# Joining two low-rank products and pairing the attention scores under a TensorE-bound MLP

## The chip, the cores and the metric

The kernel runs on one core of a Trainium2 chip. The metric is device time in microseconds (us) of one execution; "before" and "after" are compared by runs that shared a chip. In the profile PE is TensorE's matmuls, PEld its weight loads, DVE VectorE, ACT ScalarE, POOL GpSimd, and SPq/ACTq the queues that issue transfers. L545 is line 545 of the kernel before; the changed kernel keeps these numbers in all lines used here, and some experiments are six or fewer lines longer.

## The reference

Retention over four batches, then a mixer with a low-rank product over the sequence and an MLP.

```python
# q, k, v: (4, 8, 768, 64); gamma per head
state = gamma * state + k_t v_t^T;  y_t = q_t state / sqrt(64)
x = y as (4, 768, 512)
h = x^T @ U @ V            # U: 768x32, V: 32x768
u = x + h^T
out = u + relu(u @ w_ch1) @ w_ch2      # 512 -> 2048 -> 512
```

## The kernel before

The retention is computed in chunks of 128 positions. Batch b's attention is woven into batch b-1's MLP: `weave` lays the MLP's matmul pieces in order and drops other steps (turns, states, scores, mixes) between them where a share of the MLP's work is done. A step's number, such as 0.743, is such a share; steps fall in front of the first piece that begins at or after it. PSUM banks are dealt from rings, and two of the rings that matter hold a single bank.

```python
RINGS = {"mlp": [0, 1, 2], "s": [3, 4], "o": [5], "qk": [6], "st": [7], ...}

def turn_pe(nm, b, sc, xs_=(0, 1)):       # transposes q or k of two chunks
    tp = bank("qk", bf16)
    ...                                   # 4 or 8 transposes into tp (L465)
    if nm == "q": q_order(b, sc, tp)      # ScalarE (batch 1) reads the bank
    else:         evac("A", turned(...), tp[...])

def score_one(b, ci):
    score(b, ci)                          # 8 matmuls of 64 rows into s, s (L506)
    screen(b, ci)                         # VectorE: 2 masked products, a (L516)

def score_two(b, ci):
    score(b, ci + 1, ("mlp", "o"))
    score(b, ci)
    screen(b, ci + 1)
    screen(b, ci)
    ...

def mix(b, ci):
    o_p = bank("o")
    ...                                   # state part L540 (not for ci = 0), a part L545
    evac("A", xs[b][:, ci], o_p)
# ... cut ...
    grow_turned(0)                        # L861, 4 matmuls of 32 rows, then the eviction uT
    keep_busy(3)                          # 12 filler matmuls, L193
    first = [part(lr_expand, 0, 4, 2), part(lr_turn_pe, 0, 4),
             part(lr_expand, 0, 0, 4)]    # L576 matmuls and x additions, woven in
```

GpSimd prepares batch 1's k, q and v (products and casts from transfers that have landed), in a fixed order, behind its casts of the weights.

Of the kernel before, what the change touches and what calls it, by code (L numbers as in the profile page):

```python
# [18 lines left out]
def kernel(  # L19
# [52 lines left out]
    def bank(tag, dtype=fp32):  # L72
        n_bank[0] += 1
        ring = RINGS[tag]
        ring.append(ring.pop(0))
        return psum.tile([P, 2048 // (4 if dtype == fp32 else 2)], dtype,
                         tag=f"bank{ring[-1]}", name=f"{tag}_{n_bank[0]}",
                         bufs=1)
# [103 lines left out]
    idle_bank = [None]  # L182
# [385 lines left out]

    grown = {}

    def lr_grow(b, j0, nj, last="qk"):
        banks = [bank(t) for t in ("s", "s", "o", last)]
        grown[b] = banks
        for j in range(j0, j0 + nj):
            for c in range(NCB):
                nc.tensor.matmul(banks[c][:, ts(j - j0, P)],  # L576
                                 V4[ds(RK * c, RK), ts(j, P)],
                                 pcs[b][ds(RK * c, RK)], start=True, stop=True)
# [277 lines left out]
            nc.tensor.matmul(xT[c][:, ts(j, P)], xs[b][:, j, ts(c, P)], ident16,  # L856
                             start=(j == 0), stop=False, skip_group_check=True)

    def grow_turned(b):
        for c in range(NCB):  # L860
            nc.tensor.matmul(xT[c][:, :LO], pcs[b][ds(RK * c, RK)],  # L861
                             V4[ds(RK * c, RK), :LO], start=False, stop=True,
                             skip_group_check=True)
        for c in range(NCB):
            evac("AD"[c % 2], uTs[b][:, :NLO, c], four(xT[c]))

# [56 lines left out]
    for c in range(1, NCB):  # L923
        x_turn(c, 0)
        x_turn(c, 2)
    idle_bank[0] = bank("s")
    grow_turned(0)
    keep_busy(3)
    first = [part(lr_expand, 0, 4, 2), part(lr_turn_pe, 0, 4),
             part(lr_expand, 0, 0, 4)]  # L930

    prep_keys(1, pair(1, 0)[:AHEAD])
    for j in range(4):
# [1 line left out]
    for b in range(1, B + 1):  # L935
        tracks = []
        if b > 1:
            old = b - 1 < SEVEN
            first = [part(lr_expand, b - 1, 4, 2, "qk" if old else "st"),
                     part(lr_turn_pe, b - 1, 4, "qk" if old else "o")  # L940
                     if b < 3 else part(lr_turn, b - 1, 4)]
            if not old:
                RINGS["mlp"] = [6, 0, 1, 2]
        tracks.append((first, *((0.02, 0.2), (0.02, 0.14), (0.0, 0.06),
                                (0.0, 0.03))[b - 1]))
        if b < B:
            if b == 1:
                at = [0.503, 0.61, 0.675, 0.735, 0.793, 0.845]
                lag = [0.01, 0.035, 0.065]
                for sc in range(NSC):  # L950
                    keys = pair(b, sc)
                    c0, c1 = 2 * sc, 2 * sc + 1
                    if sc:
                        tracks.append(([part(prep_keys, b, keys[:AHEAD])],
                                       at[c0] - 0.1, 1))
                    tracks.append(([part(prep_keys, b, keys[AHEAD:])],
                                   at[c1] - 0.1, 1))
                    for f, d in ((part(turn_pe, "q", b, sc),
                                  at[c0] + (0.035, -0.042, -0.042)[sc]),
                                 (part(turn_pe, "k", b, sc, (0,)),  # L960
                                  at[c0]),
                                 (part(turn_pe, "k", b, sc, (1,)), at[c1])):
                        tracks.append(([f], d, d))
                for sc in range(NSC):
                    tracks.append(([part(prep_keys, 2, pair(2, sc))],
                                   0.752 + 0.03 * sc, 1))
                for i in range(2 * NSC):
                    tracks.append(([part(turn_dma, "kq"[i % 2], 2, i // 2)],
                                   0.84, 0.84))
                for f, d in zip(w2_sums(0) + w2_sums(2) + w2_sums(4),  # L970
                                (0.51, 0.525, 0.54, 0.585, 0.655, 0.67, 0.72,
                                 0.735, 0.78, 0.8, 0.875, 0.895)):
                    tracks.append(([f], d, d))
            else:
                at = [(0.205, 0.06)[b - 2] + (0.074, 0.1)[b - 2] * i
                      for i in range(NCK)]
                lag = [0.0, 0.04, 0.1]
                two = [(0.25, 0.395, 0.595), (0.1, 0.27, 0.44)][b - 2]
                if b == 2:
                    for _ in range(RING):  # L980
                        feed_one(False)
                    steps = [(0.01 + 0.022 * i, f)
                             for i, f in enumerate(w2_sums(6))]
                    steps.append((0.125, part(lr_grow, 1, 0, 4, "st")))
                    steps += [(0.125 + 0.022 * i, part(lr_add, 1, 0, 4, (c,)))
                              for i, c in enumerate((3, 2, 0, 1))]
                    for sc in range(NSC):
                        steps.append((0.57 + 0.08 * sc,
                                      part(prep_keys, 3, pair(3, sc))))
                        for nm in "kq":  # L990
                            if not sc:
                                steps.append((0.64, part(turn_dma, nm, 3, sc)))
                else:
                    steps = [(0.08, part(turn_dma, nm, 3, sc))
                             for sc in (1, 2) for nm in "kq"]
                for d, f in steps:
                    tracks.append(([f], d, d))
            if b > 1:
                for sc in range(NSC):
                    d = two[sc] - (0.04, 0.05, 0.08 if b == 2 else 0.05)[sc]  # L1000
                    tracks.append(([lambda b=b, sc=sc: q_order(
                        b, sc, live["q", b, sc])], d, d))
            for i in range(NCK):
                more = (0.027, 0.0, 0.0, 0.0, 0.0, -0.015)[i]
                late_by = (0.032, 0.0, 0.012, 0.0, 0.01, 0.0)[i]
                if b == 2 and i > 3:
                    p = two[2] + 0.05 * (i - 4)
                    steps = [(state, p - 0.035), (score_one, p),
                             (mix, p + (0.07, 0.047)[i - 4])]
                elif b > 1:  # L1010
                    p = two[i // 2]
                    steps = [(state, p + (-0.035, 0.02)[i % 2]),
                             (mix, p + (0.08, 0.12)[i % 2])]
                    if i % 2 == 0:
                        steps.append((score_two, p))
                else:
                    steps = [(state, at[i] + lag[0]),
                             (score_one, at[i] + lag[1] + more),
                             (mix, at[i] + lag[2] + late_by)]
                for f, d in steps:  # L1020
                    tracks.append(([part(f, b, i)], d, d))
            t = at[-1] + lag[2] if b == 1 else two[-1] + (0.102, 0.122)[b - 2]
            if b == 1:
                turns = [part(x_turn, c, j0, b, tag)
                         for c, tag in enumerate(("qk", "st", "s", "s"))
                         for j0 in (0, 2)]
                for fs, d in ((turns[:4], t + 0.006),
                              ([part(lr_open, b), part(lr_proj, b)], t + 0.022),
                              (turns[4:], t + 0.023),
                              ([part(grow_turned, b)], t + 0.044)):  # L1030
                    tracks.append((fs, d, d))
            else:
                for fs, d in (([part(lr_open, b), part(lr_proj, b)],
                                0.025),
                              ([part(lr_grow, b, 0, 4, "st")], 0.047),
                              ([part(lr_add, b, 0, 4, (0,))], 0.047),
                              ([part(lr_add, b, 0, 4, (1,))], 0.052),
                              ([part(lr_add, b, 0, 4, (2,))], 0.066),
                              ([part(lr_add, b, 0, 4, (3,))], 0.076),
                              ([part(lr_turn, b, 0)], 0.08),  # L1040
                              ([part(lr_turn, b, 2)], 0.081)):
                    tracks.append((fs, t + d, t + d))
        weave(b == 1, mlp_pieces(b - 1), *tracks)
# [29 lines left out]
```

## Time and profile before

| what | before |
|---|---|
| time, median of the first runs | 220.2 us (220.09 to 221.0) |
| span of the profiled execution | 218.6 us |
| TensorE busy | 211.7 us, 97% |
| VectorE, ScalarE, GpSimd busy | 66%, 42%, 38% |
| waits of TensorE, 24 to 84 us | one: first mix on VectorE |

Ends of matmuls are modelled in this profile, so I read TensorE from start to start: what an instruction costs is the distance to the next one's start. A stall is what that distance has over the plain one. A bracket such as `[0.31 <-DVE a L516]` is idle time after the modelled end, so it understates a stall.

### The profile page before, as it was taken

What the parts mean: (1) busy time and instruction counts of PE and PEld (TensorE: products, weight loads), DVE (VectorE), ACT (ScalarE), POOL (GpSimd) and SP (SyncE); (2) the same over time, 40 slices, a digit from 0 to 9 for tenths busy, and PEclk for the clock granted to TensorE, in tenths of its full rate; (3) what the DMA queues carried; (4) which work ended last, traced back from release to release, by engine and by line L of the source; (5) the groups of instructions that cost most, each with busy time, mean ns of one, the idle gap of its engine ahead of it and who ended that gap; (6) DMA issues with size and microseconds to landing.
All of it is one profiled execution on the core that took longest, in us unless ns stands there. A gap on an engine that the chain in (4) does not pass through costs nothing.

```text
span 218.6 us, 5522 instructions
## 1 busy us (share of the span) xinstructions
PE 211.7 (97%) x2239; PEld 147.3 (67%) x2239; DVE 144.3 (66%) x303; ACT 92.8 (42%) x192; POOL 82.3 (38%) x121
## 2 busy tenths in 40 slices
PE   7879999999999999999999999999999999999994
PEld 2568854486556554666788875756888856668884
DVE  6478665334478858699695856598985542867443
ACT  3347745466356424676912005867510035551000
POOL 5457888888686977000069920000000000000000
PEclk9999999999999999999999999999999999999999
DMA  5999999999999999999999789700007240000043
GB/s 166 301 293 294 319 352 276 352 356 244 219 226 220 253 230 213 161 339 250 228 236 164 175 197 182 122 1 3 0 3 181 110 135 9 3 1 0 18 153 120
DMA packets 84489, 38.82 MB, mean 178 GB/s; under 512 B 58384, under 2 KB 77552, under 8 KB 84464
## 3 DMA queue, kind: packets, MB, share of 16 engines
q1 hardware_dynamic: 83456, 36.84, 71.5%
q10 hardware_dynamic: 1008, 1.64, 2.6%
q8 instruction: 17, 0.28, 0.6%
q14 instruction: 8, 0.07, 0.1%
HBM read 27.46 MB, written 6.29 MB: 154 GB/s over the span
## 4 chain that ended last, share of the span: by engine, by line
PE 91%; ACT 3%; DMA 2%; DVE 2%; SPq 1%; issue 0%; ACTq 0%
PE mlp L763 38%; PE A L655 15%; PE mlp L814 9%; PE C L655 6%; PE B L655 4%; DMA in<-in_q_dram 2%; PE o L545 2%; PE s L506 2%; ACT qT L85 2%; PE o L540 1%; PE st L490 1%; PE mlp L193 1%; PE qk L465 1%; PE s L576 1%; PE mlp L363 1%; PE s L404 1%
## 5 line engine op out<-in xcount | busy, mean ns | idle before, releaser
L763 PE MATMUL mlp<-uT,w1b 128*128 128x512 f16 (+1 forms) x512 | 88.6, 326 | 0.0
L773 ACT ACTIVATE gT<-mlp 128x512 f16<-128x512 f32 (+1 forms) x98 | 47.4, 490 | 63.9 <-PE mlp L763 61.7
L763 PEld LDWEIGHTS <-w1b 128*128 128x128 f16 x512 | 48.2, 98 | 30.0 <-POOL w1b L340 0.2
L771 DVE TENSOR_SCALAR gT<-mlp 128x512 f16<-128x512 f32 (+1 forms) x30 | 16.7, 556 | 25.3 <-PE mlp L763 24.7
L655 PEld LDWEIGHTS <-gT 128*128 128x128 f16 x288 | 27.7, 98 | 3.3
L814 PE MATMUL mlp<-w2b,gT 128*128 128x512 f16 x96 | 23.7, 380 | 0.0
L306 POOL TENSOR_TENSOR kd<-in,gk 128x512 bf16<-128x512 f32 x18 | 19.0, 1071 | 5.5 <-DMA in<-in_k_dram 5.5
L516 DVE TENSOR_TENSOR a<-s,mask 128x512 bf16<-128x512 f32 x26 | 16.7, 683 | 6.6 <-PE s L506 6.6
L655 PEld LDWEIGHTS <-gS 128*128 128x128 f16 x200 | 19.2, 98 | 2.6
L306 POOL TENSOR_TENSOR qd<-in,gq 128x512 bf16<-128x512 f32 x18 | 18.9, 1070 | 1.0 <-DMA in<-in_q_dram 1.0
L655 PE MATMUL A<-w2t,gT 128*128 128x256 f16 x144 | 18.4, 273 | 0.0
L85 ACT ACTIVATE state<-st 64x256 bf16<-64x256 f32 x40 | 15.0, 374 | 6.2 <-PE st L386 3.2
L85 ACT ACTIVATE x<-o 128x512 f16<-128x512 f32 x20 | 11.9, 596 | 13.3 <-PE o L545 12.9
L814 PEld LDWEIGHTS <-gT 128*128 128x128 f16 x96 | 8.4, 98 | 7.9 <-issue 0.2
L304 POOL CAST vd<-in 128x512 bf16<-128x512 f32 x18 | 11.4, 649 | 1.3 <-DMA in<-in_v_dram 1.2
L346 POOL CAST w2b<-in 128x512 f16<-128x512 f32 x16 | 9.7, 613 | 1.5 <-DMA in<-in_moe_w_ch_dram 0.6
L608 POOL COPY gate<-gT 128x1 f16<-128x1 f16 x1 | 0.2, 190 | 25.5 <-DVE gT L608 25.5
L340 POOL CAST w1b<-in 128x512 f16<-128x512 f32 x16 | 9.3, 613 | 0.8 <-DMA in<-in_moe_w_ch_dram 0.4
L655 PE MATMUL B<-w2b,gT 128*128 128x256 f16 x72 | 9.3, 273 | 0.0
L655 PE MATMUL A<-w2t,gS 128*128 128x256 f16 x72 | 9.0, 273 | 0.0
L582 DVE TENSOR_TENSOR x<-s,x 128x256 f16<-128x256 f32 (+1 forms) x16 | 8.1, 550 | 1.3 <-issue 0.7
L655 PE MATMUL A<-w2b,gT 128*128 128x256 f16 x72 | 8.8, 273 | 0.0
(156 smaller groups left out, 293.3 us busy)
## 6 DMA issues: line engine op xcount, KB each, us to landing
in<-in_moe_w_ch_dram SPq DMA_DIRECT2D x32, 256.0 KB, 5.2
in<-in_k_dram SPq DMA_DIRECT2D x24, 256.0 KB, 5.4
in<-in_q_dram SPq DMA_DIRECT2D x24, 256.0 KB, 5.0
in<-in_v_dram SPq DMA_DIRECT2D x24, 256.0 KB, 5.4
out_dram<-o SPq DMA_DIRECT2D x16, 256.0 KB, 2.0
out_dram<-o ACTq DMA_DIRECT2D x6, 256.0 KB, 3.1
out_dram<-o SPq DMA_DIRECT2D x3, 128.0 KB, 1.7
Uf<-in_moe_U_dram SPq DMA_DIRECT2D x1, 96.0 KB, 5.4
```

Source lines behind the costliest of these rows:

```text
L85: nc.scalar.activation(dst, src, AF.Copy)
L304: nc.gpsimd.tensor_copy(out=t, in_=src)
L306: nc.gpsimd.tensor_tensor(t, src, g, op=ALU.mult)
L340: nc.gpsimd.tensor_copy(out=w1b[:, c, ts(mb, 512)], in_=take("w1", mb, c))
L346: nc.gpsimd.tensor_copy(out=w2b[:, m], in_=take("w2", m))
L516: nc.vector.tensor_tensor(a, four(sp[i]), causal(mask), op=ALU.mult)
L582: nc.vector.tensor_tensor(us[b][:, ds(j0, nj), ts(c, P)], four(grown[b][c])[:, :nj], xs[b][:, ds(j0, nj), ts(c, P)], op=ALU.add)
L655: nc.tensor.matmul(acc[key, i], lhs[:, m, ts(i, P)], rhs[:, m], start=(fresh and m == 0), stop=(m == NH - 1), skip_group_check=True)
L763: nc.tensor.matmul(g_p[:, :sz], w1b[:, c, ts(m, P)], uTs[b][:, ds(j, nj), c], start=(c == 0), stop=(c == NCB - 1))
L771: nc.vector.tensor_relu(gT[:, m, ds(lo, sz)], g_p[:, :sz])
L773: nc.scalar.activation(gT[:, m, ds(lo, sz)], g_p[:, :sz], AF.Relu)
L814: nc.tensor.matmul(ch, gT[:, m, ts(j, P)], w2b[:, m], start=(m == 0), stop=(m == NM - 1))
```

## The change

It is meant to take array switches (from matmuls on 128 rows to ones on 64 or 32, or back; in the trace of before 0.09 us each: eight L814 and the entry of a score take 1.82 from 53.06 to 54.88, where eight alone take 1.73) and fillers out of TensorE's sequence: batch 0's product for its last two chunks goes beside the turned product in place of the fillers, and batch 1's chunks 0 to 3 are scored in pairs. Mixes, the w2 sums (VectorE's sums of blocks of w2, with which later batches multiply) and one turn of q are moved to fit.

```diff
-    def lr_grow(b, j0, nj, last="qk"):
-        banks = [bank(t) for t in ("s", "s", "o", last)]
+    def lr_grow(b, j0, nj, last="qk", third="o"):
+        banks = [bank(t) for t in ("s", "s", third, last)]
...
-    def grow_turned(b):
+    def grow_turned(b, more=None):
...                                          # the four L861
+        if more:
+            more()
...
-    idle_bank[0] = bank("s")
-    grow_turned(0)
-    keep_busy(3)
-    first = [part(lr_expand, 0, 4, 2), part(lr_turn_pe, 0, 4),
-             part(lr_expand, 0, 0, 4)]
+    grow_turned(0, part(lr_grow, 0, 4, 2, "qk", "st"))
+    lr_add(0, 4, 2)
+    first = [part(lr_turn_pe, 0, 4), part(lr_expand, 0, 0, 4)]
...
-        tracks.append((first, *((0.02, 0.2), ...
+        tracks.append((first, *((0.06, 0.22), ...
...
                     for f, d in ((part(turn_pe, "q", b, sc),
-                                  at[c0] + (0.035, -0.042, -0.042)[sc]),
+                                  at[c0] + (0.035, -0.042, -0.05)[sc]),
...
                 for f, d in zip(w2_sums(0) + w2_sums(2) + w2_sums(4),
-                                (0.51, 0.525, 0.54, 0.585, 0.655, 0.67, 0.72,
-                                 0.735, 0.78, 0.8, 0.875, 0.895)):
+                                (0.51, 0.525, 0.54, 0.555, 0.57, 0.585, 0.6,
+                                 0.615, 0.715, 0.73, 0.745, 0.76)):
...
                     steps = [(state, at[i] + lag[0]),
-                             (score_one, at[i] + lag[1] + more),
-                             (mix, at[i] + lag[2] + late_by)]
+                             (mix, (0.702, 0.724, 0.825, 0.85, 0.88, 0.912)[i])]
+                    if i in (0, 2):
+                        steps.append((score_two, (0.652, 0, 0.775)[i]))
+                    elif i > 3:
+                        steps.append((score_one, (0.842, 0.868)[i - 4]))
```

More of the change, by code (lines that the diff above doesn't have):

```diff
@@ L943 @@
                 RINGS["mlp"] = [6, 0, 1, 2]
-        tracks.append((first, *((0.02, 0.2), (0.02, 0.14), (0.0, 0.06),
+        tracks.append((first, *((0.06, 0.22), (0.02, 0.14), (0.0, 0.06),
                                 (0.0, 0.03))[b - 1]))
@@ L1003 @@
             for i in range(NCK):
-                more = (0.027, 0.0, 0.0, 0.0, 0.0, -0.015)[i]
-                late_by = (0.032, 0.0, 0.012, 0.0, 0.01, 0.0)[i]
                 if b == 2 and i > 3:
```

## The prediction

> **What bounds the kernel now.** I read the page first (busy shares, slices, chain), then the waits of TensorE, then the timelines of the two places that the change edits: the start of batch 0's up-projection (27 to 31 us) and its down-projection, under which batch 1's attention runs (50 to 78 us).
>
> ```profile
> PE 211.7 (97%) x2239; PEld 147.3 (67%) x2239; DVE 144.3 (66%) x303; ACT 92.8 (42%) x192; POOL 82.3 (38%) x121
> ...
> PEclk9999999999999999999999999999999999999999
> ...
> PE 91%; ACT 3%; DMA 2%; DVE 2%; SPq 1%; issue 0%; ACTq 0%
> ```
>
> TensorE is busy 97% of the span at the full granted clock, and 91% of the chain is TensorE. No transfer, and no other engine for long, is between two of its instructions after the first 28 us. The waits of TensorE between 24 and 84 us are one line:
>
> ```profile
> PE o L545 <- DVE a L516: 0.3, 1, 0.3
> ```
>
> So time is saved only by taking instructions, array switches or that one wait out of TensorE's own sequence, and it is lost wherever a new wait is put in.
>
> The timeline at the start of the up-projection (start, length, engine, line, what):
>
> ```profile
> 27.60 0.84 PE L193 MATMUL s<-ones 128*128 128x128 bf16 x12
> 27.70 1.08 ACT L85 ACTIVATE uT<-mlp 128x512 f16<-128x512 f32 x2 [0.94 <-PE o L861]
> ...
> 28.34 0.68 DVE L87 CAST uT<-o 128x512 f16<-128x512 f32 x1
> 28.34 1.11 PE L763 MATMUL mlp<-uT,w1b 128*128 128x512 f16 x4
> ...
> 29.38 0.23 PE L576 MATMUL s<-pc,V 32*128 32x128 f16 x2
> ...
> 29.61 2.76 PE L763 MATMUL mlp<-uT,w1b 128*128 128x512 f16 x12
> ```
>
> The twelve fillers (L193) lie exactly beside the eviction of uT. The first real matmul starts at 28.34, when ScalarE has its first half done, and the fourth needs VectorE's last cast, which ends at 28.34 + 0.68 = 29.02. The fillers therefore cost nothing.
>
> The timeline of TensorE under the down-projection, a lone score (L506), batch 1's first mix (L545), and a turn (L465):
>
> ```profile
> 53.06 1.89 PE L814 MATMUL mlp<-w2b,gT 128*128 128x512 f16 x8
> 54.88 0.40 PE L506 MATMUL s<-qO,kT 64*128 64x128 bf16 x8
> 55.21 1.04 PE L814 MATMUL mlp<-w2b,gT 128*128 128x512 f16 x4
> 56.33 0.29 PE L545 MATMUL o<-vd,a 128*128 128x64 bf16 x4
> 56.93 0.29 PE L545 MATMUL o<-vd,a 128*128 128x64 bf16 x4 [0.31 <-DVE a L516]
> 57.06 1.03 PE L814 MATMUL mlp<-w2b,gT 128*128 128x512 f16 x4
> 57.92 0.39 PE L465 MATMUL qk<-ident,kd 128*128 128x128 bf16 x4
> 58.15 0.39 PE L490 MATMUL st<-vd,kd 128*128 128x128 bf16 x4
> ```
>
> Ends of matmuls are modelled, so I count from start to start. Four L814 take 0.87 (57.06 to 57.92 is 0.86). Eight would take 1.73, but 53.06 to 54.88 is 1.82: 0.09 goes in entering the score. The score holds 0.33, of which 0.09 is leaving it again. The mix stalled by more than the 0.31 shown: 55.21 + 0.87 = 56.08, so its first half waited 0.25, and its second began 0.60 after the first where 0.12 is needed, 0.48 more. That is **0.73 us** of waiting for VectorE.
>
> [...] about 0.09 us on each change between 128 rows and 64 or 32, both ways (53.06 to 55.21 above). [...] the screens here show 0.68 to 0.69, and follow each other every 0.60.
>
> **Part 1, the joined low-rank product.** It removes twelve fillers (free, as shown) and moves eight L576 matmuls from after the first up-projection piece to directly behind the turned product, which already has the array in 32 rows: no entry of their own, some 0.12 us, done by about 27.72. Nothing the eviction needs is changed: it still starts at 27.70. So the first piece again starts at 28.34 and its fourth matmul again at about 29.07 (29.02 and a handover of 0.05). Then the second piece follows after 0.22, at 29.29, in place of 29.61. Gain: **0.32 us** (0.09 entry, 0.14 work, 0.09 exit). The four x additions on VectorE begin 0.8 us earlier and are done by about 30.4; the turn at about 31.0 doesn't wait for them.
>
> **Part 2, scores in pairs.** Six lone scores become two pairs and two lone ones. A pair from batch 2 in this trace:
>
> ```profile
> 92.81 1.47 PE L763 MATMUL mlp<-uT,w1b 128*128 128x256 f16 x12
> 94.21 0.23 PE L506 MATMUL mlp<-qO,kT 64*128 64x128 bf16 x1
> ...
> 94.77 1.47 PE L763 MATMUL mlp<-uT,w1b 128*128 128x256 f16 x8
> ```
>
> It holds 94.77 - 94.21 = 0.56 with 0.09 of entry: 0.65, against 2 x (0.33 + 0.09) = 0.84 for two lone ones. Two pairs gain 2 x 0.2 = **0.4 us**.
>
> The old stall of 0.73 goes, but a new one comes at the same mix. The first pair stands behind the eighth down piece. VectorE first adds that piece's row (starts 0.20 after the piece's end, next start 0.60 later), then screens chunk 1 twice and chunk 0 twice at 0.60, the last taking 0.69: done at 0.20 + 0.60 + 3 x 0.60 + 0.69 = 3.29 after the piece, plus 0.05 of handover. TensorE is at the second half of the first mix after 0.65 (pair) + 0.87 + 0.22 + 0.22 (turn, state) + 0.87 + 0.12 = 2.95. Stall: 3.34 - 2.95 = **0.4 us**, if VectorE has finished its eight w2 sums by then; with the times that these show (0.41 alone, up to 1.1 beside GpSimd) they end about 0.3 us ahead. Gain against before: 0.73 - 0.4 = 0.33.
>
> **The turn of q that moved.** The instruction order of the changed program shows something that the diff hides. With its offset at -0.05, the turn of chunk pair 2's q falls in front of the same down piece as the turn of chunk 3's k: twelve L465 transposes in a row, four into the qk bank and eight into the next qk tile, which is the same single bank. The first of the eight waits for ScalarE. Before, a state and a whole down piece lay between. ScalarE's eviction of such a k turn:
>
> ```profile
> 58.34 0.60 ACT L85 ACTIVATE kT<-qk 128x512 bf16<-128x512 bf16 x1 [0.49 <-PE qk L465]
> ```
>
> The four transposes before it hold TensorE from 57.92 to 58.15; the eviction ends at 58.94, and with 0.05 for handover TensorE could go on at 58.99. So the new wait is 58.99 - 58.15 = **0.85 us**, with ScalarE free beforehand: the previous mix's eviction should end about 0.5 us earlier.
>
> I went through the rest in the new order. The second mix finds the o bank free within 0.05 of when it needs it (eviction 0.60 and 0.20 latency against a piece of 0.87). The mix of chunk 2 needs its last screen 3.0 us after its pair starts and comes 3.0 us after. Mixes 3 to 5 and scores 4 and 5 have 0.1 us or more. w2 sums done earlier on VectorE take nothing off TensorE: the row addition they used to delay at 77 us had no one waiting. GpSimd's later work (batch 2's v into buffers that the later mixes free) is held by transfers to beyond the new mixes.
>
> **Sum.** Part 1 -0.32; pairs -0.4; old stall -0.73; new stall +0.4; q turn +0.85: -0.2 us. Everything after 78 us follows TensorE and is moved by that as a whole. Predicted **220.0 us** against 220.2.
>
> **Rivals.** (a) The q wait isn't there or is mostly covered: then -1.0 us, 219.2. For it speaks that whoever moved the offset by hand will have wanted something from it; against it, that the ring has one bank and the order has nothing in between. (b) VectorE is late for the first mix: eight w2 sums now crowd into 50 to 59 us, beside GpSimd, where before they ran to 68. [...] if the crowding puts VectorE 0.5 us behind at the first pair, that lands on TensorE whole: 220.5. The second pair has VectorE idle over a microsecond before it. (c) The fillers kept the clock up[...] (d) The later shift upsets the one tight spot in batch 2 at 99 to 102 us, where the chain passes through ScalarE; worth 0.2 us either way.
>
> **Range and chances.** Runs of before spread from 220.09 to 221.0. Taking (a) and (b) as the ends and the spread of medians of about 0.3: 219.2 to 220.7. A 2% change is 4.4 us, and no part or rival reaches it. Faster by over 2%: 0.01; within: 0.98; slower: 0.01.
>
> **What would show each step.** Right on part 1: no L193 between the turned product and L763, first piece at about 28.3, second at about 29.3, PEclk still full. Right on the pairs: two groups of sixteen L506 holding 0.56. Right on the stalls: the waits of TensorE list o L545 behind VectorE's a by a few tenths, and a new line, qk L465 behind ScalarE's kT, by 0.6 to 0.8. Batch 1's last mix should start 0.2 us earlier than 76.92. The prediction is wrong if the qk wait is missing, if the first mix waits longer than 0.7 us, or if the time leaves the range for a reason after 84 us.

Passages are cut from it where a mark stands. The sum: -0.32 - 0.4 - 0.73 + 0.4 + 0.85 = -0.2 us, and the stated range rests on (a) and (b) alone. A wait for ScalarE: the trace of before has no such wait, so that the turned q must wait in full was the author's estimate, tested below. A w2 sum: in that trace the one at 66.20, with GpSimd idle, took 0.41, and those that overlapped GpSimd's work took 0.41 to 1.26, three of them 1.08 or 1.09. The handover of 0.05 can be checked there: the first mix's last screen ends at 55.59 + 1.28 = 56.87 and the matmul behind it starts at 56.93, 0.06 later.

## The result

The changed kernel took 220.93 us (median, 220.71 to 221.07) against 220.24. The ratio is 1.0023 with a 95% interval of 0.9999 to 1.0048: no change at the 2% level, as predicted, but the median lay 0.2 us above the stated range, and the sign was opposite to the forecast. Ratios here and below are the mean time of one kernel's fast runs over that of the other's of the same rounds, so they aren't quite the ratio of the medians quoted. Later, with more rounds, the changed kernel had 220.66 against 220.45.

From the page of the changed kernel, the busy times, the granted clock and the chain:

```profile
PE 210.7 (96%) x2227; PEld 146.8 (67%) x2227; DVE 144.1 (66%) x303; ACT 93.1 (43%) x192; POOL 82.5 (38%) x121
...
PEclk9999999999999999999999999999999999999999
...
PE 74%; DMA 16%; DVE 3%; ACT 2%; POOL 2%; SPq 1%; issue 1%; ACTq 0%
```

TensorE lost the twelve fillers and a microsecond of busy time, and the span still grew by 0.5 us. The chain tells where to look: TensorE's share fell from 91% to 74%, and transfers, which had 2%, have 16%. The waits of TensorE from 24 to 84 us (us in total, times, longest), one line before, are four now:

```profile
PE qk L465 <- ACT kT L85: 0.7, 1, 0.7
PE mlp L763 <- ACT uT L85: 0.6, 1, 0.6
PE qk L465 <- POOL qd L306: 0.3, 1, 0.3
PE o L545 <- DVE a L516: 0.2, 1, 0.2
```

The second of these is the gap that the fillers used to fill. The timeline of the start of the up-projection shows that nothing was lost there:

```profile
27.44 0.22 PE L576 MATMUL s<-pc,V 32*128 32x128 f16 x2
...
27.64 1.08 ACT L85 ACTIVATE uT<-mlp 128x512 f16<-128x512 f32 x2 [0.94 <-PE o L861]
...
...
28.28 2.83 PE L763 MATMUL mlp<-uT,w1b 128*128 128x512 f16 x12 [0.56 <-ACT uT L85]
```

The first matmul comes 28.28 - 27.64 = 0.64 us after the eviction's start, as before (28.34 - 27.70). Now three pieces run on without a break. Under the down-projection, TensorE's timeline:

```profile
57.43 0.28 PE L465 MATMUL qk<-ident,qd 128*128 128x128 bf16 x2
57.98 0.51 PE L465 MATMUL qk<-ident,qd 128*128 128x128 bf16 x6 [0.28 <-POOL qd L306]
...
62.02 0.28 PE L545 MATMUL o<-vd,a 128*128 128x64 bf16 x4
62.53 0.29 PE L545 MATMUL o<-vd,a 128*128 128x64 bf16 x4 [0.23 <-DVE a L516]
...
64.84 0.39 PE L465 MATMUL qk<-ident,kd 128*128 128x128 bf16 x4
65.91 0.61 PE L465 MATMUL qk<-ident,qd 128*128 128x128 bf16 x8 [0.69 <-ACT kT L85]
```

Three stalls stand here. At 65.91 the q transposes come 1.07 us after the four k transposes that need 0.22: 0.85 us for the one qk bank, as forecast. At 62.53 the mix's second half comes 0.51 after the first in place of 0.12: 0.39, as forecast. At 57.98 is one that I had not forecast: after two transposes (0.11) the q turn of chunks 2 and 3 stands for 57.98 - 57.54 = 0.44 us, waiting for GpSimd's product. In the kernel before, the same turn and GpSimd's two products were:

```profile
53.50 1.04 POOL L306 TENSOR_TENSOR qd<-in,gq 128x512 bf16<-128x512 f32 x1
...
55.55 1.04 POOL L306 TENSOR_TENSOR qd<-in,gq 128x512 bf16<-128x512 f32 x1 [1.00 <-DMA in<-in_q_dram]
```
```profile
59.23 0.61 PE L465 MATMUL qk<-ident,qd 128*128 128x128 bf16 x8
```

The product was done at 56.59 and its turn came at 59.23, 2.6 us later. In the changed kernel the product ends at 57.93 (next line) and the turn comes at 57.43:

```profile
55.52 2.41 POOL L306 TENSOR_TENSOR qd<-in,gq 128x512 bf16<-128x512 f32 x2
```

Two things met. With the join in front and the first score, the first mix and its stall taken out of the way, TensorE asks 1.8 us earlier; and GpSimd was 1.3 us later in this execution.

A fourth stall stands outside the region that changed. The MLP of batch 2 starts at 130.85. The last L576 in front of it started at 130.35, and going on takes 0.15 (130.21 to 130.36 in the trace of before); 0.35 us is waiting. The profile names VectorE:

```profile
130.85 1.02 PE L763 MATMUL mlp<-uT,w1b 128*128 128x512 f16 x4 [0.28 <-DVE o L676]
```

It can't be that addition: before, the same matmul started at 130.36, while the same addition ran from 130.25 to 130.67. The list by tile has another candidate, the second transpose of uT by transfer. After, then before:

```profile
L600 SPq DMA_TRANSPOSE uT<-x x2: 1260/2032/2804, 123.6 to 126.5; - x2
...
DMA to landing us min/median/max: 4.2/4.8/5.5
```
```profile
L600 SPq DMA_TRANSPOSE uT<-x x2: 1232/1630/2027, 123.5 to 124.8; - x2
...
DMA to landing us min/median/max: 4.8/5.1/5.4
```

Its issue began at 126.5 and it landed 4.2 later, at 130.7, just ahead of the matmul; before, it landed at 124.8 + 4.8 = 129.6. This is the likely cause, not a tested one. No other trace has this stall.

### The profile page after: what moved, and what is told of

It reads as the page before. It is cut to its first block, busy times and chain, and to the rows that moved or that the text cites. A ratio compares the mean times of both kernels' runs of the same rounds, so it can differ in the third digit from the quotient of the medians.

```text
span 219.1 us, 5501 instructions
## 1 busy us (share of the span) xinstructions
PE 210.7 (96%) x2227; PEld 146.8 (67%) x2227; DVE 144.1 (66%) x303; ACT 93.1 (43%) x192; POOL 82.5 (38%) x121
## 4 chain that ended last, share of the span: by engine, by line
PE 74%; DMA 16%; DVE 3%; ACT 2%; POOL 2%; SPq 1%; issue 1%; ACTq 0%
PE mlp L763 29%; PE A L655 15%; DMA in<-in_moe_w_ch_dram 8%; PE C L655 6%; DMA in<-in_k_dram 6%; PE mlp L814 6%; PE B L655 4%; DMA in<-in_q_dram 2%; PE o L545 2%; ACT qT L85 2%; PE o L540 2%; PE mlp L193 1%; PE st L490 1%; PE s L506 1%; DVE a L516 1%; POOL qd L306 1%
## 5 line engine op out<-in xcount | busy, mean ns | idle before, releaser
L814 PE MATMUL mlp<-w2b,gT 128*128 128x512 f16 x96 | 23.9, 380 | 0.0
L516 DVE TENSOR_TENSOR a<-s,mask 128x512 bf16<-128x512 f32 x22 | 14.1, 681 | 2.4 <-PE s L506 2.4
L814 PEld LDWEIGHTS <-gT 128*128 128x128 f16 x96 | 8.4, 98 | 7.4 <-issue 0.2
```

Source lines behind the costliest of these rows:

```text
L516: nc.vector.tensor_tensor(a, four(sp[i]), causal(mask), op=ALU.mult)
L814: nc.tensor.matmul(ch, gT[:, m, ts(j, P)], w2b[:, m], start=(m == 0), stop=(m == NM - 1))
```

## The experiments

All twelve kernels gave correct results. The first four shared a chip, so did the next four, and the last four.

| run | us, median | before, same rounds | ratio of fast runs, 95% |
|---|---|---|---|
| after_again | 220.66 | 220.45 | 1.0007 (0.9993 to 1.0021) |
| join_only | 220.24 | 220.45 | 0.9984 (0.9971 to 0.9997) |
| pairs_only | 221.13 | 220.45 | 1.0029 (1.0007 to 1.0050) |
| q2_back | 219.94 | 220.45 | 0.9970 (0.9951 to 0.9989) |
| q1_late | 220.26 | 220.43 | 0.9982 (0.9968 to 0.9997) |
| screen_first | 220.43 | 220.43 | 0.9995 (0.9970 to 1.0021) |
| all_three | 219.52 | 220.43 | 0.9951 (0.9927 to 0.9974) |
| q2_early_alone | 221.64 | 220.43 | 1.0053 (1.0038 to 1.0068) |
| all_four | 219.77 | 220.52 | 0.9959 (0.9918 to 1.0000) |
| q_load_first | 220.54 | 220.52 | 0.9993 (0.9972 to 1.0015) |
| before_no_fill | 220.41 | 220.52 | 0.9991 (0.9966 to 1.0016) |
| before_again | 220.80 (one run) | 220.52 | none |

The effects are near the scatter of whole runs, so I use the traces for the sizes. One source of scatter is the first 28 us, which wait for loads (in the trace of before, a load of q holds the chain for 4.83 us from 2.33): the eviction of uT started anywhere from 27.63 to 29.04 in these traces. So I measure each trace **from the start of that eviction to the start of the last addition on VectorE** (for before, 215.84 - 27.70 = 188.14; for the changed kernel, 216.31 - 27.64 = 188.67), and take off the stalls that depend on loads (the q turn of chunks 2 and 3 on GpSimd, and the one on the transpose). The last addition, before and then after:

```profile
215.84 0.29 DVE L716 TENSOR_TENSOR o<-B,db 128x128 f32<-128x128 f32 x1 [0.15 <-PE B L711]
```
```profile
216.31 0.29 DVE L716 TENSOR_TENSOR o<-B,db 128x128 f32<-128x128 f32 x1 [0.15 <-PE B L711]
```

| trace | distance | load stalls | rest | rest against before |
|---|---|---|---|---|
| before | 188.14 | 0 | 188.14 | |
| before_again | 188.14 | 0 | 188.14 | 0.00 |
| before_no_fill | 188.14 | 0 | 188.14 | 0.00 |
| join_only | 187.85 | 0 | 187.85 | -0.29 |
| q2_early_alone | 188.98 | 0 | 188.98 | +0.84 |
| pairs_only | 188.48 | 0.25 | 188.23 | +0.09 |
| after | 188.67 | 0.44 + 0.35 | 187.88 | -0.26 |
| after_again | 189.88 | 1.97 | 187.91 | -0.23 |
| q1_late | 188.02 | 0 | 188.02 | -0.12 |
| q_load_first | 187.89 | 0 | 187.89 | -0.25 |
| screen_first | 187.73 | 0.23 | 187.50 | -0.64 |
| q2_back | 187.80 | 0.74 | 187.06 | -1.08 |
| all_three | 186.65 | 0 | 186.65 | -1.49 |
| all_four | 186.64 | 0 | 186.64 | -1.50 |

Kernels that should have the same rest agree within 0.03 us, so the table can tell terms of 0.1 us apart where whole runs can't.

**after_again.** No edit.

> The changed kernel itself, again, for more rounds and a second trace. My theory is that two of its four visible waits are fixed by the order of the program (the q turn behind the k turn in the one qk bank, 0.85 us; the first mix behind its screens, 0.39) and come again to within 0.03 us, and that the other two (the q turn of chunks 2 and 3 on GpSimd's product, 0.44; the second batch-2 transpose by DMA, 0.35) depend on when transfers land, so may differ by several tenths in this trace. Rival: all four are fixed and the loss of 0.5 to 0.7 us repeats. Theory: 0.0 to 0.7 us over before; rival: 0.5 to 0.7.

Its times ran from 220.38 to 222.19, wider than before's 220.29 to 221.01. The profiled execution was the slowest, and TensorE's timeline shows why; GpSimd's product follows it:

```profile
56.67 1.03 PE L814 MATMUL mlp<-w2b,gT 128*128 128x512 f16 x4
58.44 0.28 PE L465 MATMUL qk<-ident,qd 128*128 128x128 bf16 x2 [0.74 <-POOL qd L306]
59.62 0.51 PE L465 MATMUL qk<-ident,qd 128*128 128x128 bf16 x6 [0.90 <-POOL qd L306]
```
```profile
57.16 2.40 POOL L306 TENSOR_TENSOR qd<-in,gq 128x512 bf16<-128x512 f32 x2
```

The down piece ends its turn at 57.54; TensorE then stands 0.90 us for the product's first half and 1.07 for its second, 1.97 in all. The other two stalls are again 0.39 and 0.85. The theory holds: two are fixed, the one on GpSimd moves between executions, and the one at 130 us did not come again.

**join_only.** The join on the kernel before.

```diff
-    idle_bank[0] = bank("s")
-    grow_turned(0)
-    keep_busy(3)
+    grow_turned(0, part(lr_grow, 0, 4, 2, "qk", "st"))
+    lr_add(0, 4, 2)
```

> The joined low-rank product alone, the scores as before. My theory: the second up-projection piece begins 0.32 us earlier against the turned product and everything behind follows, so 0.3 us less than before (219.9 if before is 220.2). Rival: without the fillers the clock drops or the eviction is late[...]; granted clock under 9 tenths in the slices around 28 us would show it.

0.9984, and -0.29 us in the trace: the theory, with a granted clock of 0.999 in the profiled execution. This trace says one more thing. GpSimd was late here too, and TensorE, asking at the old time, hardly noticed; GpSimd first, then TensorE:

```profile
57.11 2.22 POOL L306 TENSOR_TENSOR qd<-in,gq 128x512 bf16<-128x512 f32 x2
```
```profile
59.25 0.65 PE L465 MATMUL qk<-ident,qd 128*128 128x128 bf16 x8
```

The product ended at 59.33. The changed scoring, asking at 57.4 to 57.9, would have stood for about 1.5 us, as an estimate from these times.

**pairs_only.** The change with the old low-rank lines put back (the diff above reversed).

> The scores in pairs with the q turn and the sums moved as in the change, the low-rank product and the fillers as before. My theory: pairs -0.38, old mix wait -0.72, new mix wait +0.39, q turn behind k turn +0.85, and 0 to +0.45 for GpSimd's q product according to the transfers: 0.15 to 0.6 us slower than before. Rival (the scoring gains what was meant and the loss lies in the join): 0.3 to 0.7 us faster than before.

1.0029, with 0.25 us on GpSimd in its trace (eight transposes took 0.86 where 0.61 is plain) and +0.09 for the rest: the scoring half gained nothing as it was placed. The rival is out.

**q2_back.**

```diff
-                                  at[c0] + (0.035, -0.042, -0.05)[sc]),
+                                  at[c0] + (0.035, -0.042, -0.042)[sc]),
```

> The change with the q turn of chunks 4 and 5 back at its old offset, so that one down piece lies between it and the k turn. My theory: the wait of qk L465 on ScalarE's kT is gone from the waits of TensorE and the time is 0.85 us under the changed kernel's, about 0.3 us under before. Rival (the wait only moves on to the next thing that holds TensorE, such as the score pair behind it): under 0.3 us less than the changed kernel.

The line for ScalarE's kT is gone from the waits, and the rest is 187.06 against 187.9, 0.83 us less. The profiled execution had 0.74 on GpSimd; its six runs split, three at 219.3 to 219.6 and three at 220.3 to 220.4.

**q2_early_alone.** The same line the other way round, in the kernel before.

> The kernel before with only the offset of the q turn of chunks 4 and 5 changed to -0.05. My theory: this alone puts twelve L465 in a row and adds 0.85 us of waiting for ScalarE's kT in the one qk bank: 0.85 us over before. Rival (the wait only stands in for the one on VectorE's screens that would follow anyway): 0 to 0.3 us over before.

+0.84 us in the trace, and these are all its waits of TensorE from 24 to 84 us:

```profile
PE qk L465 <- ACT kT L85: 0.7, 1, 0.7
PE o L545 <- DVE a L516: 0.3, 1, 0.3
```

Whole runs gave 1.0053, about 1.2 us, with an interval (0.8 to 1.5) that holds the 0.84. The second line is the old stall, untouched, so the new one was not in place of another.

**q1_late.**

```diff
-                                  at[c0] + (0.035, -0.042, -0.05)[sc]),
+                                  at[c0] + (0.035, -0.02, -0.05)[sc]),
                                  (part(turn_pe, "k", b, sc, (0,)),
-                                  at[c0]),
+                                  at[c0] - (0.0, 0.042, 0.0)[sc]),
```

> The change with the q turn of chunks 2 and 3 one down piece later, behind the first score pair, and the k turn of chunk 2 in the place it leaves; nothing else moved. My theory: the wait of qk L465 on GpSimd's qd (0.44, 1.97, 0.25 and 0.74 us in the four traces that have it, mean 0.85) goes or shrinks to 0 to 0.6 us because TensorE asks for qd 1.5 us later, and the waits of 0.85 (ScalarE's kT) and 0.39 (VectorE's a) stay: 0.3 to 0.9 us under the changed kernel, about as before. Rival (the late qd is not what costs; the scatter of the runs is): no difference beyond 0.2 us from the changed kernel.

The wait on GpSimd is gone; the q turn came at 59.26, and the product had ended at 56.57 + 2.40 = 58.97. The median is 0.2 us under before. The first mix waits 0.47 here (0.39 elsewhere) and starts 0.05 late besides, which is all of the 0.13 by which this rest is higher than the changed kernel's. TensorE has no less work in front of it; VectorE was late. Its row addition began at 59.18 with no idle time before it, directly behind a w2 sum that took 1.26 us beside GpSimd's product, where in the changed kernel VectorE had been idle for 0.44. So rival (b) of the prediction showed up here.

**q_load_first.**

```diff
+        if b == 1 and sc == 1:
+            return [*qs, ("k", b, i), ("v", b, i), ("k", b, i + 1),
+                    ("v", b, i + 1)]
```

> The change with batch 1's q of chunks 2 and 3 loaded and multiplied ahead of the k of chunk 2, nothing else moved. It asks whether lateness on GpSimd and its loads is what the q turn waits for: if so, the product ends about 1.1 us earlier, and the wait of qk L465 on GpSimd's qd, 0.25 to 2.0 us in the traces so far, falls to 0 to 0.9; mean 0.4 to 0.8 us under the changed kernel. Rival (the wait follows TensorE's own place, not the load): unchanged.

In the trace the turn of q doesn't wait, although it comes as early as in the changed kernel:

```profile
57.77 0.61 PE L468 MATMUL qk<-ident,qd 128*128 128x128 bf16 x8
```

But this is weaker than it looks. Loads landed early in the profiled execution (the last w2 cast ended at 49.6 us, as in the first trace of before, 49.5), and with the old order the product might have been in time too. And the median, 220.54 against 220.52, is not the 0.4 to 0.8 us under the changed kernel that I expected (0.1 under after_again, on another chip). The run is inconclusive. That lateness of the product is what TensorE waits for rests on the ends of the waits: they come 0.05 to 0.06 us after the product in both traces of the changed kernel (57.93 and 57.98, 59.56 and 59.62), and on q1_late, where the wait is gone.

**screen_first.**

```diff
+        if b == 1:
+            score(b, ci, ("mlp", "o"))
+            score(b, ci + 1)
+            screen(b, ci)
+            screen(b, ci + 1)
+            return
```

> The change with chunk 0 (and 2) scored and screened before chunk 1 (and 3) in batch 1's pairs, its second half in the o bank, so that the first mix has its screens 1.2 us earlier. My theory: the 0.39 us wait of o L545 on VectorE's a is gone from the waits, the others stay, and the time is 0.4 us under the changed kernel. Rival (the second mix or the o bank takes the wait over): under 0.15 us less, with a new line of waits for o.

The wait of the first mix is gone, no other came in its place, and the rest is 0.39 us under the changed kernel's. Whole runs (219.69 to 221.47) are too scattered to show it.

**all_three.** q2_back, q1_late and screen_first together.

> All three repairs together: q turn of chunks 4 and 5 at its old offset, q turn of chunks 2 and 3 later, the first screens first. My theory: of before's sequence it has 0.32 (join) + 0.38 (pairs) + 0.72 (old wait of the mix) = 1.4 us less and no new wait, so 219.0 if before is 220.4, and no line over 0.2 us in the waits of TensorE from 50 to 78 us other than a possible one on GpSimd's last q product. Rival: with TensorE ahead, the next thing that comes by transfer (q of chunks 4 and 5) takes over as the wait, and it gains 0.5 us or less on before.

TensorE's waits from 24 to 84 us are one line, the gap of the former fillers:

```profile
PE mlp L769 <- ACT uT L85: 0.6, 1, 0.6
```

The rest is 186.65: 1.49 us under before, and 1.24 under the changed kernel, which is 0.85 + 0.39. One of its six runs was slow (222.92 at clock 0.992) and is left out of the ratio, 0.9951. **It beats the kernel before by about half a per cent**, which is under the 2% level but clear of its interval. The changed kernel wasn't run in these rounds; in its own two sets it stood at 1.0023 and 1.0007 of before.

**all_four.** all_three with the q turn of chunks 4 and 5 at offset 0.0 and the k turn of chunk 4 0.033 earlier.

> The three repairs, and the q turn of chunks 4 and 5 two down pieces later (the k turn of chunk 4 two pieces earlier, in its place), so that it too has slack to GpSimd's product. My theory: the runs of all_three near 220.0 beside those near 218.9 come from the waits of the q turns on GpSimd when transfers land late; with more slack fewer runs are high, and the mean of the fast runs is 0.2 us under that of all_three, 219.0 if before is 220.4; no wait over 0.25 us between 50 and 78 us. Rival (the spread comes from elsewhere, such as the first 28 us): the same spread and mean as all_three, 219.3, or more where a new wait on ScalarE (qO behind kT) comes up.

The same rest, 186.64, and no gain in the mean or the scatter (218.63 to 221.75). Its profiled execution took 220.26 with no stall at all: its uT eviction started at 29.04 where all_three's started at 27.63. The difference of 1.41 is that between the two profiled times (220.26 - 218.88 = 1.38). This fits the rival, that the scatter left here comes from the loads of the first 28 us, but it is one pair of executions; the others weren't traced.

**before_no_fill.**

```diff
     grow_turned(0)
-    keep_busy(3)
```

> The kernel before without its twelve fillers and with nothing in their place. My theory: the fillers lay beside the eviction of uT, so nothing changes: within 0.1 us of before, the first up-projection matmul again 0.64 us after the eviction's start, the granted clock full. Rival (the fillers kept the clock up, or the tail of the fillers delayed the first piece): 0.1 us or more in either direction.

188.14 exactly, and 0.9991 with an interval on both sides of 1: the fillers cost nothing and gave nothing. TensorE idled 0.7 us in their place, and the granted clock of the profiled execution was 1.0. It was 1.0 too in after_again, where TensorE idled 0.90 us at 59.6, and in the first trace of before, where it idled 0.85 at 16.0.

**before_again.** No edit.

> The kernel before, for a second trace. My theory: the load of batch 1's q for chunks 2 and 3 lands at times that differ by a microsecond or two between executions, and the trace that I predicted from was at the early end (product done at 56.6 us against 57.2 to 59.6 in eight others); here the product ends between 56.6 and 59.5, and its turn at 59.2 still doesn't wait. Rival (the change itself makes the loads late): the product ends at 56.6 again within 0.2.

```profile
55.87 2.04 POOL L306 TENSOR_TENSOR qd<-in,gq 128x512 bf16<-128x512 f32 x2 [1.78 <-DMA in<-in_q_dram]
```

The product ended at 57.91, 1.3 us later than in the first trace of the same program, after a wait for the load. So the first trace of before, from which I predicted, was at the early end. The rival is out.

## Why the prediction was wrong

**The bound.** Right: TensorE's sequence sets the time, and every term below is a sum over it.

**Part 1.** Right. -0.32 predicted, -0.29 measured alone; the fillers free, the granted clock 0.999 (join_only) and 1.0 (before_no_fill).

**Pairs, old stall, first mix, q turn.** Right, term by term. A pair in the changed kernel enters and leaves as in batch 2 (0.55 us from its first score to the next down matmul, 59.29 to 59.84, against 0.56); the old stall is gone; the first mix waits 0.39 (0.4 predicted); the q turn waits 0.85 (0.85), shown twice, by taking it out of the change (-0.83) and putting it into before (+0.84). One reading under it was loose: in the trace of before, no turn waits for ScalarE, which was done at least 0.29 us ahead of each turn under the down-projection; that trace showed the order and not a wait. The changed kernel's shows it: there ScalarE's eviction ends at 65.26 + 0.60 = 65.86 and the turn comes at 65.91. The sum of these terms with part 1 was -0.2; the two traces of the changed kernel have -0.26 and -0.23 without the load stalls.

**The step that failed** is the sentence "I went through the rest in the new order". It goes through mixes, scores, w2 sums and later work on GpSimd, and has no term for the wait of a q turn on GpSimd's product. In the one trace of before, the q turn of chunks 2 and 3 would have had a small margin at its new place: 57.5, where the changed kernel asks, against a product done at 56.6. But the product ended between 56.6 and 59.6 us in the traces that load in the old order, and the trace I held was the earliest of them. A wait that comes by transfer was not among my rivals either, although the change had just spent 1.8 of 2.6 us of slack there.

The term that was missing measured 0.44, 1.97, 0.25, 0.74 and 0.23 us in the five traces that ask at the new time in the old load order, 0.73 on average. Added to -0.25 it would make the changed kernel some 0.5 us slower than before, with more scatter. This is rough: one of the five is the slowest of its kernel's runs. Whole runs gave medians 0.7 and 0.2 higher in two sets of rounds, and both intervals include 1.

In the profiled execution, batch 1's last mix, forecast 0.2 us before 76.92, started at 77.06, and the 0.44 lies in front of it. The 0.35 at 130 us, probably the transpose and seen once, makes up the rest: -0.26 + 0.44 + 0.35 = +0.53, against 188.67 - 188.14. (This sum closes because -0.26 is what the other two leave; the check is that it agrees with the forecast of -0.2.) So one sign of being wrong that the prediction named, a reason after 84 us, came up too: without the 0.35 this execution, 220.87, would have been inside the range. The other three runs weren't traced.

**Rivals.** (a) fell: the q wait is there in full. (b), VectorE late for the first mix, did not show in the changed kernel, where VectorE was idle for 0.44 and 2.37 us before its row addition; it did in q1_late, and cost 0.13 us. (c) fell with before_no_fill, whose granted clock was 1.0 without the fillers. (d) did not show: near 100 us, the last MLP matmul and the first score after it start 0.32 or 0.33 us apart in all fourteen traces.

**Left open.** Whether the change itself makes GpSimd later. In the old load order, the two q products took 2.40 to 2.41 us together in seven of the eight traces with the moved w2 sums (2.22 in all_three), and 2.04 to 2.22 in the four with the sums in the old places where they ran back to back. In the first trace of the changed kernel two of the sums lie beside them (1.08 and 1.26 us each, 0.41 when alone). That is argued from overlap, not tested alone, and it would be 0.4 us of the lateness at most. On average the second product ended at 58.4 us in those eight traces and at 57.8 in the five with the sums in the old places, each group spread over 2.4 us or more, so this settles nothing. Also open is why the issue of the first of the two uT transposes took anywhere from 1.2 to 2.8 us in these traces. A late issue alone isn't enough for the stall at 130 us: in before_no_fill the second transpose was issued at 126.41, about as in the changed kernel's first trace, and landed at 129.72, in time.

## What to carry to other kernels

When a change takes work out of the bound engine's sequence, list everything that now gets asked for earlier, and compare its slack with the spread of arrival over several traces (56.6 to 59.6 us here, against a slack of 0.8 in the changed kernel by the one trace), not with its arrival in one. Two steps that share a one-bank ring need other work between them (0.85 us here without it); look for it in the instruction order, since offsets in a schedule don't show it. Where effects are a few tenths in 220 us, measure between two marks in the trace that leave out the scattered start.
